# Attention and two MoE layers on one core: another order of the first loads, and the softmax sums' 1e-9 added by a tensor_reduce over pairs

## The chip, the cores and the metric

One core of a Trainium2 chip runs the whole program; nothing is shared with another core. The metric is the device time of one execution in microseconds. The kernel before takes 882.75 us, the median of three runs (882.33 to 882.92). The engines are named as in the profile: PE is TensorE (PEld its weight loads), DVE is VectorE, ACT is ScalarE, POOL is GpSimd, and SP is the queue from which all DMAs of this kernel are issued.

## The reference, cut to what matters

`q`, `k` and `v` are 4 x 8 x 576 x 64 (batch, heads, tokens, head width), in float32. For each batch and head two attentions are added: one over tokens averaged in fours, repeated back, and one local, in which a token sees the tokens less than 4 away. Both use the same softmax:

```python
s = s - np.max(s, axis=-1, keepdims=True)
a = np.exp(s)
a = a / (np.sum(a, axis=-1, keepdims=True) + 1e-09)
```

The sum, as 2304 rows of 512, goes through two layers; the weights come as 8-byte floats (512 x 2048 and 2048 x 512 for each layer):

```python
h = x @ w_in
g = h * (1.0 / (1.0 + np.exp(-h)))      # second layer: exp(-1.702 * h)
x = g @ w_out
```

## The kernel before

The work is cut into steps. Each step is a small function that issues a few instructions of one engine, with a name, an engine and what it reads and writes. The class `Plan` (from line 100) derives from that which steps must come before which. The order in which the steps are issued isn't worked out while building: it is the string `PLACES`, two characters a step, with the place of every step. `placed` (L135) refuses places that contradict the dependences and sorts the steps by them. So each engine's instruction order, and that of the SP queue, is the one written in `PLACES`; an engine runs its instructions in that order and waits where an operand isn't there. "Soft" edges (`plan.soft`) are no dependences: they are passed over in that test. A second table, `ON`, says for some steps on which engine they run.

**Attention.** The 2304 tokens are 8 blocks `m` of 288 (half a batch each). A unit `u` is one block and one pair of heads `hp`, so 32 units, four to a block. In order, a unit of the first blocks has these steps (from L1182; names as in the order, then the lines of the profile): `lk` and `lqqraw` load keys and queries (L1051, two DMAs each; in later batches L1048, four DMAs each), `vw` loads windows of the values (L1097) after POOL has zeroed the edge of the first one (`zvw0.0`), `KT` and `QT` form transposed and pooled keys and queries on TensorE with a helper tile `four` (L1131, L1195), ACT copies them (`KC` L1136 and L1138, `QC` L1199), `SC` makes the scores (L1219, L1226), `DM` and `LC` take maxima and cap the local scores (L1234, L1241, L1244), `LS` subtracts the maximum (L1250, on POOL or DVE), `DE` and `LE` take exponentials on ACT (L1256, L1260), `LU` sums the local ones (L1263), `RC` adds 1e-9 and takes reciprocals (L1267, L1268), `LN` and `DN` multiply by them (L1278 on POOL or DVE; L1275 on DVE or L1273 on ACT), `TP`, `TC` and `PT` transpose (L1285, L1289, L1293), `VP` and `VC` sum the values in fours (L1170, L1174), `AV` multiplies with the values (L1302, L1308), and `UC`, `XA`, `XM` copy, add and take the row's largest value (L1314 to L1326). In later batches DVE transposes keys and queries instead (`KX` L1141, `QX` L1204). The sums of one unit stand in a tile `smr` of 128 x 8: six columns from `LU`, two from the accumulators of `DE`.

**Weights of layer one** come in pairs of 1 MB (`ldst1in.c.j`, `ldst1out.c.j`, L524) into four staging tiles, 8 pairs in and 8 out. A pair is made into float32 by `ca` and `cz` on ACT (L326, L330), `cs` on DVE (a shift, L334), `sg` (the sign: on DVE a mask, L339, or on ACT a copy, L347) and two `cp` (the low words added, 512 columns each, on POOL or DVE, L351); `sps` and `spm` find its scale (L563, L578), and `hi` and `lo` split it into two float16 parts (L379, L383).

**Layers.** A block `m` is scaled and split (`rm`, `am`, `pw`, `xh`, `xl`; L769 to L784), then come eight pairs of h steps of 12 matmuls (L709), tanh and the rest on ACT and DVE (L721 to L734), and the output products (L842 in block 0, L814 after it). Layer two does the same for 9 blocks of 256 rows (L876 to L955); its sums `gs2` (L895 to L897) run on POOL or DVE as `ON` says. The weights of layer two are loaded and converted during layer one.

**Around the change.** The list `first` at the end (L1494) ties the first loads together with soft edges in the order that is written there. In `PLACES`, SP's order before is: weight pair in.0.0, queries 0, keys 0.0, queries 1, keys 0.1, value windows 0.0, pairs in.1.0 and in.0.2, queries 2, keys 0.2, windows 0.1, pair in.1.2, keys 0.3, pair in.2.0, and so on. TensorE begins with `QT0 KT0.0 QT1 SC0 KT0.1 VP0.0 SC1 TP0 AV0`. On POOL the initialisation (L997) sets constants to memory ahead of everything else.

## Time and profile before

| | |
|---|---|
| median of three runs | 882.75 us |
| the profiled execution | 885.88 us, its span 884.1 us |
| instructions | 23833 |
| PE busy | 859.8 us (97%) |
| DVE busy | 606.7 us (69%) |
| ACT busy | 465.4 us (53%) |
| POOL busy | 152.8 us (17%) |
| mean granted TensorE clock | 0.985 of full speed |

The profiled execution is one run by itself, timed with the profiler on. Its span goes from the first instruction to the last. Shares of busy time are averages over stages with different limits: PE is full from 132 us on and not before, so a stage must be read from its own stretch of the trace.

### The profile page before, as it was taken

Reading aid. Unit: us, or ns where it says so; the run is one execution under the profiler, and the core shown is the slowest. Engines: PE = TensorE matmul, PEld = TensorE weight load, DVE = VectorE, ACT = ScalarE, POOL = GpSimd, SP = SyncE. Lnnn points to the kernel's source line nnn. Section 1 sums busy time; section 2 is a strip of 40 time slices with the busy share of each in tenths; the row PEclk is TensorE's granted clock in tenths of the full one; section 3 lists DMA queues with packets and bytes.
Section 4 is the critical chain, followed back from the end, with each engine's and each line's share of the span. In section 5 each row is a group of like instructions: output and inputs, shape, how many; then the busy total and the mean of one; then the engine's idle time right before and its main releaser. Section 6 shows DMA issues by size and latency. Waiting matters only on the chain.

```text
span 884.1 us, 23833 instructions
## 1 busy us (share of the span) xinstructions
PE 859.8 (97%) x10212; PEld 718.1 (81%) x10212; DVE 606.7 (69%) x1342; ACT 465.4 (53%) x824; POOL 152.8 (17%) x184
## 2 busy tenths in 40 slices
...
GB/s 250 290 144 244 161 116 109 48 104 161 125 86 149 119 131 76 167 80 108 120 18 293 97 1 1 24 1 1 26 26 13 13 13 2 36 2 24 1 18 32
DMA packets 114990, 75.86 MB, mean 86 GB/s; under 512 B 94788, under 2 KB 100292, under 8 KB 113860
## 3 DMA queue, kind: packets, MB, share of 16 engines
...
## 4 chain that ended last, share of the span: by engine, by line
PE 84%; DVE 8%; ACT 4%; DMA 2%; SPq 1%; issue 1%; DVEq 0%; ACTq 0%
PE hps L876 20%; PE ops L814 19%; PE hps L709 19%; PE oy L955 10%; PE oz L955 5%; PE ox L955 2%; PE ul L1308 2%; PE sl L1226 1%; DMA kraw<-in_k_dram 1%; PE sl L1219 1%; PE ul L1302 1%; PE ops L842 1%; SPq L1051 1%; DVE wout L383 1%; DVE g L904 1%
## 5 line engine op out<-in xcount | busy, mean ns | idle before, releaser
L709 PE MATMUL hps<-xhl,win 128*128 128x288 f16 x1536 | 198.1, 287 | 0.9 <-DVE tg L724 0.9
L876 PE MATMUL hps<-xhl,win 128*128 128x256 f16 x1728 | 190.3, 273 | 0.0
L876 PEld LDWEIGHTS <-win 128*128 128x128 f16 x1728 | 169.1, 98 | 19.6
L709 PEld LDWEIGHTS <-win 128*128 128x128 f16 x1536 | 148.3, 98 | 38.3 <-issue 1.0
L814 PE MATMUL ops<-g,wout 128*128 128x288 f16 x1344 | 170.9, 286 | 0.0
L955 PEld LDWEIGHTS <-g 128*128 128x128 f16 x1512 | 147.7, 98 | 19.4 <-DVE g L904 1.3
L814 PEld LDWEIGHTS <-wout 128*128 128x128 f16 x1344 | 129.8, 98 | 32.7 <-issue 0.6
L888 ACT ACTIVATE tg<-hps,blk 128x512 f32<-128x512 f32 x72 | 49.5, 687 | 127.6 <-PE hps L876 116.3
L891 DVE SCALAR_TENSOR_TENSOR tg<-tg,hps 128x512 f32<-128x512 f32 x72 | 49.2, 683 | 59.9 <-ACT tg L888 59.9
L904 DVE SCALAR_TENSOR_TENSOR g<-tg,g 128x896 f16<-128x896 f32 x72 | 77.4, 1086 | 0.6 <-ACT g L901 0.3
L955 PE MATMUL oy<-wout,g 128*128 128x256 f16 x648 | 75.1, 272 | 0.0
L901 ACT ACTIVATE g<-tg 128x896 f16<-128x896 f32 x72 | 67.3, 944 | 14.5 <-DVE tg L897 10.4
L721 ACT ACTIVATE tg<-hps,blk 128x576 f32<-128x576 f32 x64 | 47.2, 737 | 42.3 <-PE hps L709 34.5
L351 POOL TENSOR_TENSOR cs<-cs,cz 128x512 int32<-128x512 int32 x32 | 41.9, 1316 | 154.9 <-DVE cs L334 54.8
L724 DVE SCALAR_TENSOR_TENSOR tg<-tg,hps 128x576 f32<-128x576 f32 x64 | 47.7, 747 | 27.3 <-ACT tg L721 27.2
L895 POOL TENSOR_TENSOR tg<-tg 128x128 f32<-128x128 f32 x14 | 9.7, 691 | 293.6 <-DVE tg L891 264.1
L933 ACT ACTIVATE o<-oy,blk 128x256 f32<-128x256 f32 x27 | 12.7, 472 | 73.6 <-PE oy L955 73.6
L734 DVE SCALAR_TENSOR_TENSOR g<-tg,gs,g 128x576 f16<-128x576 f32 x56 | 46.7, 839 | 6.1 <-ACT g L731 6.0
L326 ACT ACTIVATE st<-st 128x512 f32<-128x512 f32 (+1 forms) x48 | 39.6, 831 | 20.0 <-DMA st<-in_moe_w_out_dram 11.5
L731 ACT ACTIVATE g<-tg,gs 128x576 f16<-128x576 f32 x56 | 42.7, 769 | 13.1 <-DVE tg L724 12.5
L351 POOL TENSOR_TENSOR x<-x,z 128x512 int32<-128x512 int32 x26 | 37.4, 1453 | 49.3 <-DVE x L334 28.4
L939 DVE SCALAR_TENSOR_TENSOR o<-oy,blk,o 128x256 f32<-128x256 f32 x9 | 4.4, 484 | 59.0 <-PE oy L955 34.6
...
## 6 DMA issues: line engine op xcount, KB each, us to landing
...
```

The costliest lines, as they stand in the source:

```text
L351: eng.tensor_tensor(out=s, in0=s, in1=zget()[:, o], op=ALU.add)
L709: nc.tensor.matmul(o, T[w][:, kc, a, fc * P:(fc + 1) * P], T[xk][:, kc, b, :T_], start=(n == 0), stop=(n == 3 * KC - 1))
L721: ACT.activation(out=T[tg], in_=T[ps][:, :, :T_], func=AF.Tanh, scale=T["a" + bk][:, c:c + 1])
L724: DVE.scalar_tensor_tensor(out=T[tg], in0=T[tg], scalar=1.0, in1=T[ps][:, :, :T_], op0=ALU.add, op1=ALU.mult)
L734: DVE.scalar_tensor_tensor(out=T[g][:, 1], in0=T[tg], scalar=gs, in1=T[g][:, 0], op0=ALU.mult, op1=ALU.subtract)
L814: nc.tensor.matmul(o, w[:, j, a, dc * P:(dc + 1) * P], g[:, b, j % 2, :], start=(n == 0), stop=(n == 3 * NF - 1))
L876: nc.tensor.matmul(o, T[w][:, kc, a, fc * P:(fc + 1) * P], T[xk][:, kc, b, :], start=(n == 0), stop=(n == 3 * KC - 1))
L888: ACT.activation(out=four(), in_=T[ps][:, 0, :], func=AF.Tanh, scale=T["a" + bk][:, c:c + 1])
L891: DVE.scalar_tensor_tensor(out=four(), in0=four(), scalar=1.0, in1=T[ps][:, 0, :], op0=ALU.add, op1=ALU.mult)
L901: ACT.activation(out=T[g][:, 0], in_=T[tg], func=AF.Copy, scale=GS2)
L904: DVE.scalar_tensor_tensor(out=T[g][:, 1], in0=T[tg], scalar=GS2, in1=T[g][:, 0], op0=ALU.mult, op1=ALU.subtract)
L955: nc.tensor.matmul(T[bank[acc]], g[:, a, slot, :], w, start=first and p == p0 and i == 0, stop=prod in (2, 3, 4) and p == NF // 2 - 1 and ...
```

## The change

The change has three parts. `PLACES` is a new string, and the soft edges of the first loads are gone, so SP's order at the start is now: keys 0.0, queries 0, queries 1, keys 0.1, weight pairs in.0.2 and in.0.0, value windows 0.0, pair in.1.0, queries 2, keys 0.2, windows 0.1, queries 3, pairs in.1.2 and in.2.0, keys 0.3, and so on; the places of all 2670 steps are new with it. TensorE begins with `KT0.0 QT0 SC0 KT0.1 QT1 SC1 TP0 VP0.0 AV0`. The table `ON` is new: 88 steps change their engine, among them `sg`, `cp`, `LS`, `LN`, `DN` and `gs2` steps. And `RC` adds the 1e-9 otherwise: `smr` becomes 128 x 8 x 2 with 1e-9 in the second column of each pair, a tensor_reduce adds the pairs into a new tile `smi`, and the reciprocal is taken there. `LN` and `DN` read `smi`. Two more small memsets stand in the initialisation.

```diff
--- before.py
+++ after.py
@@ -23,17 +23,16 @@
 GS1, GS2 = 2.0 ** -15, 2.0 ** -19
 BAND = 4
 ON = {
-    "DVE": ("sg1.in.0.0 sg1.in.1.0 sg1.in.2.2 sg1.in.3.0 sg1.out.0.0 sg1.out.1.0 LS0 LN0 LN2 LS4 LN5 LN8 LS9 LS10 LN10 LS13 "
-             "LN13 LN14 LN16 LS17 LN17 LN18 LS19 LN19 LS20 LN20 LS21 LS22 LS23 LN23 LS24 LS27 LS28 LS29 LN29 LS31 gs2.0.1 "
-             "gs2.0.2 gs2.0.3 gs2.0.5 gs2.1.1 gs2.1.2 gs2.1.3 gs2.1.4 gs2.1.5 gs2.1.6 gs2.2.0 gs2.2.1 gs2.2.5 gs2.3.1 "
-             "gs2.3.2 gs2.3.3 gs2.3.4 gs2.3.5 gs2.3.6 gs2.4.1 gs2.4.2 gs2.4.3 gs2.4.4 gs2.4.5 gs2.4.6 gs2.5.0 gs2.5.1 "
-             "gs2.5.2 gs2.5.3 gs2.5.4 gs2.5.5 gs2.5.6 gs2.6.1 gs2.6.2 gs2.6.5 gs2.7.0 gs2.7.1 gs2.7.2 gs2.7.3 gs2.7.4 "
-             "gs2.7.5 gs2.7.6 gs2.8.0 gs2.8.1 gs2.8.2 gs2.8.3 gs2.8.4 gs2.8.5 gs2.8.6"),
-    "POOL": ("cp1.in.0.0a cp1.in.0.2b cp1.in.1.0a cp1.in.1.0b cp1.in.1.2b cp1.in.2.0a cp1.in.2.2a cp1.in.2.2b cp1.in.3.0a "
-             "cp1.in.3.0b cp1.in.3.2a cp1.in.3.2b cp1.out.0.0a cp1.out.0.0b cp1.out.0.2a cp1.out.1.0a cp1.out.1.0b "
-             "cp1.out.1.2a cp1.out.1.2b cp1.out.2.0a cp1.out.2.2a cp1.out.2.2b cp1.out.3.0a cp1.out.3.0b cp1.out.3.2a "
-             "cp1.out.3.2b"),
-    "ACT": ("DN2 DN4 DN5 DN6 DN7 DN8 DN11 DN12 DN13 DN15 DN17 DN20 DN21 DN22 DN30 DN31"),
+    "DVE": ("sg1.in.0.0 sg1.in.0.2 sg1.in.1.0 sg1.in.1.2 sg1.in.2.0 sg1.in.2.2 sg1.in.3.2 sg1.out.0.2 sg1.out.2.0 LS0 LN0 "
+             "LS2 LN2 LS3 LN3 LS4 LN4 LS8 LS9 LN9 LN10 LS11 LS12 LN13 LS14 LS15 LS17 LS19 LN19 LN22 LN23 LN24 LN27 LS28 LS29 "
+             "LS30 LN30 LN31 gs2.0.0 gs2.0.2 gs2.0.3 gs2.0.5 gs2.1.1 gs2.1.2 gs2.1.3 gs2.1.4 gs2.1.5 gs2.1.6 gs2.2.0 gs2.2.1 "
+             "gs2.2.2 gs2.2.3 gs2.2.4 gs2.2.5 gs2.2.6 gs2.3.1 gs2.3.2 gs2.3.3 gs2.3.4 gs2.3.5 gs2.3.6 gs2.4.1 gs2.4.5 "
+             "gs2.5.1 gs2.5.2 gs2.5.3 gs2.5.4 gs2.5.5 gs2.5.6 gs2.6.1 gs2.6.2 gs2.6.3 gs2.6.4 gs2.6.5 gs2.6.6 gs2.7.1 "
+             "gs2.7.5 gs2.8.1 gs2.8.2 gs2.8.3 gs2.8.4 gs2.8.5 gs2.8.6"),
+    "POOL": ("cp1.in.0.2a cp1.in.1.0b cp1.in.1.2b cp1.in.2.0b cp1.in.2.2a cp1.in.2.2b cp1.in.3.0b cp1.out.0.0b cp1.out.0.2a "
+             "cp1.out.0.2b cp1.out.1.0a cp1.out.1.0b cp1.out.1.2a cp1.out.1.2b cp1.out.2.0a cp1.out.2.0b cp1.out.2.2a "
+             "cp1.out.3.0a cp1.out.3.0b cp1.out.3.2a cp1.out.3.2b"),
+    "ACT": ("DN3 DN4 DN5 DN6 DN7 DN8 DN9 DN10 DN11 DN12 DN13 DN14 DN15 DN16 DN22 DN24 DN25"),
 }
 
 
@@ -46,46 +45,46 @@
 PLACES = (
-    "0206040307050k0h0L0V00090n111u010a080J0q0U0Y180f0H0S0N0W0X1o1s0e0w0B0F0Q101C1I0K1r1v1y1z1B1R1V0T1Z1L262g2i2r2x1q2d2n2h2G2o2L2R1S2N2Z2Q"
...
+    "0006010204030t0f160S05090y1d1w080z0w0I0H0U111b070N0Y0T18101h1v0b0R1c1e1f1g1l1p0X1t1K1x231C272b121N1R1T1Y2c2j2q1k2f292m2A2o2E2P2a2Q2U2V"
...
 )
@@ -1011,9 +1010,11 @@
         T["qTs"] = [ac.tile([P, HALF + PD], F32, name=f"qT{i}") for i in range(2)]
         for t in T["qTs"]:
             POOL.memset(t[:, HALF:], 0.0)
-        T["smr"] = [ac.tile([P, 8], F32, name=f"smr{i}") for i in range(2)]
+        T["smr"] = [ac.tile([P, 8, 2], F32, name=f"smr{i}") for i in range(2)]
+        T["smi"] = [ac.tile([P, 8], F32, name=f"smi{i}") for i in range(2)]
         for t in T["smr"]:
-            POOL.memset(t, 1.0)
+            POOL.memset(t[:, :, 0], 1.0)
+            POOL.memset(t[:, :, 1], 1e-9)
         T["vsum"] = ac.tile([P, 3, PD], F32, name="vsum")
         POOL.memset(T["vsum"], 0.0)
         T["four"] = ac.tile([P, TT + 2 * QB], F32, name="four")
@@ -1254,28 +1255,28 @@
             T[sr] = T["smr"][u % 2]
             for hh in range(2):
                 ACT.activation(out=T[pd][:, hh, :], in_=sd()[:, hh, :], func=AF.Exp, bias=T[nmx][:, hh:hh + 1],
-                               scale=SCD if blocked(m) else 1.0, accum_out=T[sr][:PD, 6 + hh:7 + hh])
+                               scale=SCD if blocked(m) else 1.0, accum_out=T[sr][:PD, 6 + hh, 0:1])
 
         def lexp():
             ACT.activation(out=scu(), in_=scu(), func=AF.Exp, scale=0.125)
 
         def lsum():
-            DVE.tensor_reduce(out=T["smr"][u % 2][:, 0:6], in_=scu(), axis=AX.X, op=ALU.add)
+            DVE.tensor_reduce(out=T["smr"][u % 2][:, 0:6, 0], in_=scu(), axis=AX.X, op=ALU.add)
 
         def rec():
 
-            DVE.tensor_scalar(out=T["smr"][u % 2], in0=T["smr"][u % 2], scalar1=1e-9, scalar2=None, op0=ALU.add)
-            DVE.reciprocal(out=T["smr"][u % 2], in_=T["smr"][u % 2])
+            DVE.tensor_reduce(out=T["smi"][u % 2], in_=T["smr"][u % 2], axis=AX.X, op=ALU.add)
+            DVE.reciprocal(out=T["smi"][u % 2], in_=T["smi"][u % 2])
 
         def dnorm():
             if on(f"DN{u}", "DVE") == "ACT":
                 for hh in range(2):
-                    ACT.activation(out=T[pd][:, hh, :], in_=T[pd][:, hh, :], func=AF.Copy, scale=T[sr][:PD, 6 + hh:7 + hh])
+                    ACT.activation(out=T[pd][:, hh, :], in_=T[pd][:, hh, :], func=AF.Copy, scale=T["smi"][u % 2][:PD, 6 + hh:7 + hh])
                 return
-            DVE.tensor_tensor(out=T[pd], in0=T[pd], in1=T[sr][:PD, 6:8].unsqueeze(2).to_broadcast([PD, 2, 2 * PD]), op=ALU.mult)
+            DVE.tensor_tensor(out=T[pd], in0=T[pd], in1=T["smi"][u % 2][:PD, 6:8].unsqueeze(2).to_broadcast([PD, 2, 2 * PD]), op=ALU.mult)
 
         def lnorm():
-            (POOL if on(f"LN{u}", "POOL") == "POOL" else DVE).tensor_tensor(out=scu(), in0=scu(), in1=T["smr"][u % 2][:, 0:6].unsqueeze(2).to_broadcast([P, 6, 32]), op=ALU.mult)
+            (POOL if on(f"LN{u}", "POOL") == "POOL" else DVE).tensor_tensor(out=scu(), in0=scu(), in1=T["smi"][u % 2][:, 0:6].unsqueeze(2).to_broadcast([P, 6, 32]), op=ALU.mult)
 
         def dtr():
             T[tps] = bank1("tps")
@@ -1339,7 +1340,7 @@
         add(f"LS{u}", on(f"LS{u}", "POOL"), 0.58 if on(f"LS{u}", "POOL") == "POOL" else dve(192) + 0.02, lsub, lock=on(f"LS{u}", "POOL") == "DVE", r=[], w=[sc])
         add(f"LE{u}", "ACT", act(192), lexp, w=[sc])
         add(f"LU{u}", "DVE", dve(192), lsum, r=[sc, (sr, "d")], w=[sr])
-        add(f"RC{u}", "DVE", 0.34, rec, r=[(sr, "d")], w=[sr])
+        add(f"RC{u}", "DVE", 0.35, rec, r=[(sr, "d")], w=[sr])
         add(f"LN{u}", on(f"LN{u}", "POOL"), 0.55 if on(f"LN{u}", "POOL") == "POOL" else dve(192) + 0.02, lnorm, lock=on(f"LN{u}", "POOL") == "DVE", r=[sr], w=[sc])
         nby = on(f"DN{u}", "DVE")
         add(f"DN{u}", nby, dve(4 * PD) if nby == "DVE" else 2 * act(2 * PD, 1), dnorm, r=[sr], w=[pd], lock=nby == "DVE")
@@ -1490,15 +1491,6 @@
             s.deps.setdefault(s3, False)
 
 
-    by = {s.name: s for s in plan.steps}
-    first = []
-    for hp, p in zip(range(NHP), ("0.0", "0.2", "1.0", "1.2")):
-        first += [f"lk0.{hp}", f"lqqraw{hp}", f"vw0.{hp}", "ldst1in." + p]
-    first += ["ldst1in." + p for p in ("2.0", "2.2", "3.0", "3.2")]
-    for c in range(NC):
-        first += [f"ldst1out.{c}.0", f"lqqraw{NHP + c}", f"ldst1out.{c}.2"]
-    for a, b in zip(first, first[1:]):
-        plan.soft.append((by[a], by[b]))
     order = plan.placed(PLACES)
     es0 = ExitStack()
     with es0, es1, es2:
```

## Rows read from the trace of the kernel before

**Rows 1.** Busy time by stretches (start:end, length, engines' us and instructions, granted clock, DMA).

```profile
0.00:21.95 21.95, 14.18 (x156) 12.54 (x157) 6.64 (x25) 10.55 (x19) 2.55 (x25) 1.00 1.06 250
21.95:36.00 14.05, 12.98 (x222) 11.68 (x223) 9.97 (x26) 9.30 (x17) 4.30 (x5) 0.64 1.09 297
36.00:61.40 25.40, 20.09 (x320) 18.02 (x319) 22.29 (x59) 25.40 (x43) 10.72 (x9) 0.74 0.59 188
61.40:132.00 70.60, 64.90 (x1053) 50.43 (x1047) 68.12 (x160) 61.70 (x105) 33.05 (x28) 0.97 0.73 173
132.00:868.00 736.00, 734.86 (x8357) 614.38 (x8355) 498.36 (x1073) 356.70 (x638) 102.20 (x119) 1.00 0.24 66
48.00:55.10 7.10, 3.46 (x79) 2.81 (x77) 5.96 (x18) 7.10 (x15) 4.48 (x5) 0.98 0.72 206
55.10:65.60 10.50, 10.47 (x146) 8.09 (x145) 8.89 (x27) 10.16 (x18) 4.23 (x4) 0.53 0.62 150
```

**Rows 2.** The timeline from 0 to 24 us (start, length, engine, line, instruction).

```profile
0.74 0.44 SPq L524 DMA_DIRECT2D st<-in_moe_w_in_dram  x1
1.24 0.96 SPq L1051 DMA_DIRECT2D qraw<-in_q_dram  x2
...
4.21 0.18 DVE L1029 TENSOR_SCALAR four<-four 128x24 f32<-128x24 f32 x1
...
6.88 1.61 PE L1195 MATMUL qps<-four,qraw 96*128 96x120 f32 x6 [6.88 <-DMA qraw<-in_q_dram]
...
21.95 0.48 PE L1302 MATMUL ul<-pdT,vd 72*64 72x72 f32 x8 [0.89 <-ACT vd L1174]
```

**Rows 3.** DMA issues of the keys (count, size, us from issue to landing).

```profile
kraw<-in_k_dram SPq DMA_DIRECT2D x48, 72.0 KB, 4.3
```

**Rows 4.** Groups by line (shapes, count, busy us, mean ns, idle before).

```profile
L1275 DVE TENSOR_TENSOR pd<-pd,smr 72x288 f32<-72x288 f32 x16 | 9.1, 569 | 0.3
...
L347 ACT ACTIVATE z<-st 128x1024 f16<-128x1024 f32 x10 | 13.7, 1369 | 0.1
...
L339 DVE TENSOR_SCALAR z<-st 128x1024 uint16<-128x1024 uint16 x6 | 4.5, 747 | 0.0
...
L351 DVE CUSTOM_DVE_ANT_0 x<-x,z 128x1024 uint16<-128x1024 uint16 x6 | 4.6, 761 | 0.0
...
L1250 DVE TENSOR_TENSOR sc<-sc,mx 128x192 f32<-128x192 f32 x16 | 5.9, 367 | 0.3
...
L1234 DVE TENSOR_REDUCE nm<-sl 72x2 f32<-72x288 f32 x32 | 14.2, 443 | 15.0 <-PE sl L1226 15.0
...
L1241 DVE TENSOR_TENSOR sc<-sl,cap 128x192 f32<-128x192 f32 x32 | 11.0, 344 | 14.4 <-PE sl L1226 13.5 <-ACT pd L1256 0.8
...
L334 DVE TENSOR_SCALAR x<-st 128x1024 int32<-128x1024 int32 x16 | 12.5, 788 | 0.6 <-ACT st L326 0.6
```

**Rows 5.** Single lines of DVE (durations in ns: least/median/longest, first and last start).

```profile
L1263 DVE TENSOR_REDUCE smr<-sc x32: 308/344/354, 15.8 to 422.4; 128x6 f32<-128x192 f32 x32
L773 DVE TENSOR_REDUCE blk<-rm x17: 110/154/163, 57.5 to 788.9; 128x1 f32<-128x4 f32 x17
L1267 DVE TENSOR_SCALAR smr<-smr x32: 152/172/1250, 18.3 to 423.4; 128x8 f32<-128x8 f32 x32
L1278 DVE TENSOR_TENSOR sc<-sc,smr x14: 345/356/2100, 19.1 to 402.5; 128x192 f32<-128x192 f32 x14
```

**Rows 6.** The timelines of DVE and of POOL around 107 us.

```profile
107.12 1.25 DVE L1267 TENSOR_SCALAR smr<-smr 128x8 f32<-128x8 f32 x1
...
104.98 3.35 POOL L351 TENSOR_TENSOR x<-x,z 128x512 int32<-128x512 int32 x2 [3.86 <-ACT z L347]
```

**Rows 7.** Busy time of L1267 alone (DVE busy, count).

```profile
61.40:132.00 70.60, 2.54 (x6) 0.97 0.73 173
```

**Rows 8.** The timeline of PE, two h steps of twelve matmuls.

```profile
61.41 3.06 PE L709 MATMUL hps<-xhl,win 128*128 128x288 f16 x12
...
71.93 1.64 PE L709 MATMUL hps<-xhl,win 128*128 128x288 f16 x12
```

More of the change, by code (lines that the diff above doesn't have):

```diff
@@ new lines @@
+    "3130383d282J2B332N3b3u3y15171o1B1E1L1J1P1U212t2L2x2z2M2W373R3h3j3v454y502i3r3U3B473J3P4d4i353F3z403N4o4v4s4A39424g4a5g5l5t5r5z3A4O5R4T"
+    "5Z5T5W696f4j4Z53585b6m6A6w6N4n596b5m6K6s6y6S6Y5p6l6Z6D726H6P7d7v65787G7l7K7q7x7Q7V5h5U6g6r6x6G62646O776U706X797e7n7w7F7E7M7T7Z80878Q0a"
+    "0d0C0L0c0e0g0i0j0l0k0m0p0q0r0s0A0D0v0O0W0Z140h0o1q1y0n0u0x0E0B0G0F0J0K0M0Q0P1j1n0V1A1D1F1G191i1W24131a1m1r1s1z1u1I1O1Q1S1X22261V2h2p2s"
+    "2G1M202v2H1H1Z252e2g2k2n2r2u2w2C2y2D2I2F2K2O2R2S2X32363e3n3l3W4c3Q636o7j8s2d2l2Z3m2T2Y343c3f3i3k3p3t3x3C3D3H3L3K3T41444x3g3o3q3G3E3O3I"
@@ new lines @@
+    "3S3V3Z434e4l4r4w4F4N4P6d464b4f4p4B4u4E4K4X5a5f5d5j5o5u5D5M5P5S4R52565q5e5x5k5v5E5I5O5N5V5X5Y61686c6h6k6p747C7J8hcz543a6j493s5Q7B4W6a8M"
+    "847p6B99905G5A674I4G4J6e6n6v6q6C6E6V737u7b7h7m7y7H7R7U9i4k4C8k5C5H6J7f6T7o898c8d8g8w8i8n8q8x8F8J8L9Q7c7z8Y7P7Y828p8b8t8e8r8y8z8G8K8S8V"
+    "949c9l9p9s8m8H9r8C8D8O8T958X9a9b9d9e9g9n9v9x9t9C9G9I9Ja1a8adanawatak888E8R9O8P929K9V9Sa09U9Wa4a6abaaaeazaiaDaHaKaM9k9ma7agauaxaCaOaTaY"
+    "bib1b6babjbobubxbCa9alaSb9b5bhbbbfbnbpc2bwbHbKc5c6cccecwarbEbGbNbIbRbMbObVbXc0cdchcncacpcucvcycOcScUcZdmd0hP7g9Xbdc19Zc9cWb3bvdAcsclaX"
```

70 lines of the change are left out of this document (31 added, 39 removed).

## The prediction

> **What bounds the kernel now.** I read the busy time by stretches first [rows 1], then the first microseconds in order of time [rows 2, 3], then the groups by line [rows 4], and last the spread of the instructions that the new sums touch [rows 5 to 7]. From 132 to 868 us TensorE is busy for 734.86 of 736.00 us [rows 1]. The changed lanes of units 12 to 31 and of layer two lie in that stretch; TensorE's own work hides them, and the most they could uncover is the 1.1 us that it still waits. So the change is decided before 132 us.
>
> There are three stretches. Up to 21.95 us, where the first attention-times-value matmul starts, the DMA engines are full (share 1.06) and DVE works 6.64 us; TensorE starts only at 6.88 us, when the first query tile has landed behind a weight pair of 1 MB issued ahead of it [rows 1, 2]. From 36 to 61.4 us, where the first h matmul starts, ACT is busy for 25.40 of 25.40 us, DVE for 22.29 and TensorE for 20.09 [rows 1]. From 61.4 to 132 us DVE is busy for 68.12 of 70.60 us, and TensorE waits 5.7 us in all [rows 1]. Thus the early bound is loads, then ACT, then DVE, and TensorE after that.
>
> **The loads.** The first eleven loads are the same set in both orders: three query tiles, three key tiles, two value windows and three weight pairs. Only their order inside the first 22 us differs, and with the DMA engines full to 36 us [rows 1] the set lands no sooner. What changes is that the keys and queries of two units, eight DMAs on SP, go ahead of the first 1 MB pair. TensorE then begins with the key product. It can start when its helper tile "four" is written, on which the last small instruction ends at 4.39 us [rows 2], or when the keys land: the second key DMA would be issued where the second issue of the queue now stands, at 1.24 us [rows 2], and a key DMA takes 4.3 us to landing [rows 3], which gives 5.5 us. That median is one among other traffic, and here nothing is ahead in the queue, so I take 5.0 us, 1.9 us sooner; the bounds are 4.4 (2.5 us sooner) and 6.88 (nothing).
>
> Most of that is given back. Before, the copies of the first two query products lie beside key matmuls. After, the order on TensorE is keys, query, scores for unit 0, and for unit 1 the query comes last again, so each scores step waits for the copy of a product that TensorE has just made. The one such wait that the trace shows cost 0.89 us [rows 2]; at 0.75 us each, two cost 1.5 us. The TensorE steps up to 21.95 us are otherwise the same nine. Stretch one: -1.9 + 1.5 = **-0.4 us**, between -1.6 and +1.0.
>
> The weight conversions that used to run from about 6 us wait for pairs issued some 4 us later. ACT, which does the first of them, is busy for 10.55 of the first 21.95 us [rows 1] and covers that; without the cover one pair's two passes would come late. Further on SP issues the third output-weight pair ahead of two key tiles (eight DMAs) and one value tile. The keys of the second batch are first turned by DVE much later in the new order too, so I cost this at nothing; if it showed, it would be as a DVE turn waiting for a key tile. The zeroing of one value window moves behind the POOL initialisation, and two small memsets are added there: nothing, as SP reaches that window's load later.
>
> **The lanes up to 61.4 us.** ACT loses four sign copies (L347, 1369 ns) and gains one: -4.1 us [rows 4]. That is off the engine that bounds the stretch. But DVE gains them as sign masks (L339, 747 ns): four more, +3.0 us. It takes over five halves of the low-word add from POOL and gives back two (L351, 761 ns): +2.3 us. Two subtractions (L1250, 367 ns) and one local normalisation (0.36 us at its median [rows 5]) come from POOL: +1.1 us. One direct normalisation goes each way. Last, unit 4's maximum, cap, cap maximum and subtraction now stand ahead of the split of the first x tile, and one shift of an output weight behind it: 0.44 + 0.34 + 0.34 + 0.37 - 0.79 = +0.7 us [rows 4, 5] (the cap maximum by the reduce of the same width). DVE has 7.1 us more to do by 61.4 us. Its idle time from 21.95 to 61.4 us is 4.1 + 3.1 = 7.2 us [rows 1], beside what unit 0 frees earlier. So ACT stops being the bound and DVE becomes it, with next to no slack. I take **0 us** for this stretch: the 4.1 us off ACT can be cashed only as far as DVE comes early. Bounds: -4.1 (all of ACT's relief) and +4.4 (under rival one).
>
> **The lanes from 61.4 to 132 us.** DVE, the bound here, has one sign mask less (-0.75), two halves of the add more (+1.5), two local normalisations out and one in (-0.36), one subtraction in (+0.37), one direct normalisation out to ACT (L1275, -0.57), and the 0.7 us that moved ahead: **-0.5 us** [rows 4, 5].
>
> **The sums.** L1267 adds 1e-9 with a tensor_scalar; its replacement is a tensor_reduce that reads 16 numbers a partition and writes 8. The nearest rows are the reduce of 4 numbers (median 154 ns) and the reduce of 192 (344 ns) [rows 5]; 1 ns a number puts it at 0.17 us. L1267 has a median of 172 ns too, so the arithmetic costs the same. But it has stretched to 1250 ns, where L1263 has never exceeded 354 [rows 5]: at 107.12 us it lasted 1.25 us and ended with a POOL add that had run since before [rows 6]. From 61.4 to 132 us the six of them take 2.54 us [rows 7]; six at 0.17 are 1.02. So up to 1.5 us leave DVE. The wait needn't vanish, though: a DVE multiply with two inputs has stretched as well (L1278, median 356, longest 2100 ns [rows 5]), and if the POOL add is still running, the next such instruction waits instead. Between the two stands at least the reciprocal, and the POOL add runs down meanwhile; I take 1.2 of the 1.5 us, nearer to the row of the reduces that never stretched: **-1.2 us**, bounds 0 and -1.5.
>
> The Trainium skill, SBUF — State Buffer, section Who interferes with whom, has a rule for this that cuts both ways: on this chip a tensor_reduce never contends with GpSimd, while a DVE instruction with two SBUF inputs waits for a GpSimd instruction that reads SBUF. The trace agrees with both halves: 354 against 2100 ns at the longest. By the second half the wait is only handed on, and the gain in the sums would be near 0 in place of 1.2 us.
>
> **Sum.** -0.4 + 0 - 0.5 - 1.2 = -2.1 us. The profiled execution took 885.88 us around a span of 884.1; it stands 3.1 us above the median of 882.75. Taken from that median: 880.65, so **880.6 us**. About 0.2%, 1.8 us, is what a measurement of this kernel can tell from no change.
>
> **Rival one: DVE takes over before the first h matmul (slower).** Place: from the shift of weight pair 1.2 to the split of the first x tile. Of the added steps these stand behind that point: three masks, one half of the add net, one subtraction, one normalisation and the 0.7 us of unit 4, in all 2.24 + 0.76 + 0.37 + 0.36 + 0.7 = 4.4 us [rows 4, 5]; DVE's idle time from 36 us on is 3.1 us [rows 1]. For: those idle pieces are waits for ACT and TensorE and can't all be filled. Against: unit 0 comes earlier and POOL's slow adds no longer stand ahead of the conversions. Price: with none of that idle time of use, the first h matmul comes 4.4 us later, less the 1.7 us of the last stretch and the 0.4 of the first: +2.3, 885.0 us. It decides once that matmul is more than 3.9 us late (2.1 + 1.8).
>
> **Rival two: nothing to measure.** The first eleven loads are one set, TensorE's early start is eaten by the copies, and the wait of the sums is handed to the next two-input instruction. Then -0.4 - 0.5 = -0.9 at best and some lateness on DVE against it: 882.4 us. That is also the case in which the new sums change nothing.
>
> **Rival three: the clock.** From 55.1 to 65.6 us the granted clock is 0.53, close to the lower level of 1.2 GHz; before that, from 48 to 55.1 us, it was 0.98 (2.4 GHz) and TensorE was busy for 3.46 of 7.10 us only [rows 1]. With ACT relieved, those pauses may shrink and the clock hold. The twelve matmuls of an h step took 3.06 us there and 1.64 later [rows 8]; the stretch holds 10.47 us of TensorE work, and all of it at that ratio would give back 4.9 us. I take 3 for the part that the clock limits; with the forecast's sum that makes 877.6 us. Against: more DVE work means waits of TensorE elsewhere.
>
> **How the numbers follow.** Forecast 0.32 and clock 0.12: faster 0.44. Nothing: 0.31. DVE takes over: 0.25. The range is 876.5 to 885.5: it takes in the clock case below and the DVE case above, and leaves out the ends of several bounds at once. As cases of both signs hold the chance, the forecast's own range is 878.8 to 881.0.
>
> **What would show it.** Right: TensorE's first matmul near 5 us, with two new waits of 0.7 to 0.8 us ahead of scores; the first attention-times-value matmul within 1 us of 21.95; the first h matmul within 1.5 us of 61.4; ACT with pauses from 36 to 61.4 us and DVE with less idle; the sums' instruction at 0.17 us in every one of 32 cases; TensorE's waits from there to 132 us down from 5.7 to about 4. Wrong: a first h matmul over 3 us away from 61.4 either way (then DVE or the clock decided), a reduce over 0.4 us, or new waits of TensorE after 132 us.

## The result, and the profile after

The changed kernel takes 887.73 us, the median of seven runs (885.39 to 890.61), beside 882.92 us for seven runs of the kernel before on the same chip (882.33 to 885.68): a ratio of 1.0055, 95% interval 1.0040 to 1.0069. It is 4.8 us slower, where 2.1 us less was forecast; it lies beyond the upper end of the range (885.5) and on the side of rival one.

The profiled execution took 887.04 us around a span of 885.2. That of before stood 3 us above its median, so a second profile of it (run a1: 883.34 us median, profiled span 882.2) is used beside the first from here on.

The busy time by stretches, changed kernel (columns as in [rows 1]):

```profile
0.00:21.95 21.95, 15.80 (x220) 13.74 (x221) 9.51 (x32) 10.66 (x23) 5.28 (x29) 1.00 0.96 238
21.95:36.00 14.05, 10.48 (x177) 9.12 (x177) 12.31 (x29) 9.35 (x19) 3.36 (x2) 0.88 1.10 270
36.00:61.40 25.40, 17.77 (x312) 15.26 (x312) 24.68 (x59) 22.46 (x39) 8.11 (x5) 0.70 0.79 224
61.40:132.00 70.60, 66.44 (x1042) 51.80 (x1041) 67.84 (x161) 59.20 (x99) 25.81 (x25) 0.94 0.70 166
132.00:868.00 736.00, 733.60 (x8348) 613.94 (x8347) 491.08 (x1056) 358.56 (x643) 114.22 (x134) 1.00 0.24 66
```

Against [rows 1], ACT from 36 to 61.4 us went from 25.40 to 22.46 us and DVE from 22.29 to 24.68: the full engine changed, as the lanes say. TensorE lost 2.3 us of work in that stretch. And behind 132 us it now waits 2.40 us in place of 1.14.

The timeline of TensorE in the changed kernel, its start and four marks:

```profile
4.29 2.89 PE L1132 MATMUL kps<-four,kraw 96*128 96x120 f32 x12 [4.29 <-DVE four L1029]
...
9.06 0.76 PE L1220 MATMUL sl<-kd,qT 64*72 64x144 f32 x4 [0.61 <-ACT qT L1200]
...
15.27 0.76 PE L1220 MATMUL sl<-kd,qT 64*72 64x144 f32 x4 [0.64 <-ACT qT L1200]
...
20.16 0.48 PE L1303 MATMUL ul<-pdT,vd 72*64 72x72 f32 x8 [0.51 <-ACT vd L1175]
...
62.06 3.06 PE L708 MATMUL hps<-xhl,win 128*128 128x288 f16 x12
...
133.92 3.10 PE L841 MATMUL ops<-g,wout 128*128 128x288 f16 x24 [0.72 <-DVE x L855]
...
136.86 1.63 PE L708 MATMUL hps<-xhl,win 128*128 128x288 f16 x12
...
156.36 0.47 PE L1220 MATMUL sl<-kd,qd 64*72 64x144 f32 x4 [0.86 <-DVE xf L1324]
```

The start answers to [rows 2] (4.29 against 6.88 us), the matmul with the values too (20.16 against 21.95), the first h step to [rows 8] (62.06 against 61.41).

Four times divide the span: the first matmul with the values (AV), the first h matmul, the second block's first h matmul, the end. All are read from the timelines; stretches are their differences.

| kernel | AV | AV to first h | first h to second block | second block to end | span |
|---|---|---|---|---|---|
| before, first profile | 21.95 | 39.46 | 75.63 | 747.06 | 884.10 |
| before, second profile (a1) | 22.42 | 37.18 | 75.60 | 746.98 | 882.18 |
| changed | 20.16 | 41.90 | 74.80 | 748.37 | 885.23 |
| changed, old sums (a3) | 21.37 | 42.85 | 74.79 | 749.51 | 888.52 |

Against the second profile of before the changed kernel gains 2.3 us up to AV, loses 4.7 from there to the first h matmul, gains 0.8, and loses 1.4 at the end: +3.1 us in the spans.

The last three differences aren't loss and gain alone, since two of the marks have other work on either side in the two orders. The new order does the scores of unit 5 ahead of the first h matmul, the old one behind it; the new order does one unit's value products behind the second block's first h matmul, the old one ahead of it. TensorE in the changed kernel, and below it in a1:

```profile
60.68 0.76 PE L1220 MATMUL sl<-kd,qT 64*72 64x144 f32 x4 [0.78 <-ACT qT L1200]
...
138.42 0.48 PE L1303 MATMUL ul<-pdT,vd 72*64 72x72 f32 x8
138.83 0.71 PE L1309 MATMUL ul<-PT,vw 32*64 32x24 f32 x48
...
62.02 0.47 PE L1219 MATMUL sl<-kd,qT 64*72 64x144 f32 x4
62.42 0.62 PE L1226 MATMUL sl<-kT,qT 64*32 64x32 f32 x48
...
134.15 0.48 PE L1302 MATMUL ul<-pdT,vd 72*64 72x72 f32 x8
```

In a1 these scores take 62.97 - 62.02 = 0.95 us and the value products 135.20 - 134.15 = 1.05 us. So 0.95 of the 4.7 us is work that only stands earlier, the gain of 0.8 stands against 2.0 us less work and is a loss of 1.2, and 1.05 of the last 1.4 us is work that only stands later. What TensorE waits in a stretch says the same without this shift (stretches as above, changed kernel and a1; TensorE's busy time is the first figure behind the length):

```profile
20.16:62.06 41.90, 30.59 (x595) 26.43 (x595) 39.26 (x91) 34.26 (x58) 12.25 (x8) 0.77 0.91 239
62.06:136.86 74.80, 69.91 (x1031) 54.46 (x1027) 71.87 (x170) 61.26 (x107) 27.66 (x26) 0.95 0.67 155
...
22.42:59.60 37.18, 30.67 (x543) 27.43 (x543) 32.15 (x83) 34.77 (x59) 14.84 (x13) 0.75 0.84 244
59.60:135.20 75.60, 70.68 (x1139) 54.68 (x1135) 72.94 (x174) 62.53 (x110) 34.20 (x30) 0.97 0.69 165
```

From AV to the first h matmul TensorE waits 11.3 us in place of 6.5, from there to the second block 4.9 in both (there the granted clock is 0.95 in place of 0.97), and behind it 5.0 in place of 4.4. So most of the loss is in the stretch for which I had put 0 us. What is late there is DVE. Its groups by line from 20 to 62 us, the changed kernel (count, busy us, mean ns, idle before):

```profile
L333 DVE TENSOR_SCALAR x<-st 128x1024 int32<-128x1024 int32 x7 | 7.2, 1027 | 0.0
L382 DVE SCALAR_TENSOR_TENSOR win<-x,bin,win 128x1024 f16<-128x1024 f32 x5 | 6.7, 1346 | 0.0
L350 DVE CUSTOM_DVE_ANT_0 x<-x,z 128x1024 uint16<-128x1024 uint16 x7 | 5.8, 833 | 0.2
L338 DVE TENSOR_SCALAR z<-st 128x1024 uint16<-128x1024 uint16 x6 | 5.4, 899 | 0.1
```

and the same groups in the second profile of before:

```profile
L383 DVE SCALAR_TENSOR_TENSOR win<-x,bin,win 128x1024 f16<-128x1024 f32 x5 | 7.0, 1421 | 0.6 <-ACT win L379 0.6
L334 DVE TENSOR_SCALAR x<-st 128x1024 int32<-128x1024 int32 x9 | 6.4, 725 | 0.6 <-ACT st L326 0.6
L351 DVE CUSTOM_DVE_ANT_0 x<-x,z 128x1024 uint16<-128x1024 uint16 x4 | 3.2, 805 | 0.0
L339 DVE TENSOR_SCALAR z<-st 128x1024 uint16<-128x1024 uint16 x3 | 2.3, 751 | 0.0
```

The counts are about those of the prediction: three masks and three additions more by 62 us (and two shifts fewer). But a shift takes 1027 ns on the mean, where it took 725, and a mask 899 for 751. The timelines show why; DVE and, below it, POOL in the changed kernel:

```profile
25.38 0.68 DVE L350 CUSTOM_DVE_ANT_0 x<-x,z 128x1024 uint16<-128x1024 uint16 x1
25.98 1.75 DVE L333 TENSOR_SCALAR x<-st 128x1024 int32<-128x1024 int32 x1
...
44.39 1.75 DVE L333 TENSOR_SCALAR x<-st 128x1024 int32<-128x1024 int32 x1
...
25.63 1.55 POOL L350 TENSOR_TENSOR x<-x,z 128x512 int32<-128x512 int32 x1 [4.03 <-DVE z L338]
...
42.21 3.37 POOL L350 TENSOR_TENSOR x<-x,z 128x512 int32<-128x512 int32 x2 [11.86 <-DVE z L338]
```

POOL's addition ends at 25.63 + 1.55 = 27.18 us, the shift at 27.73; at 42.21 + 3.37 = 45.58, the shift at 46.14. Both shifts end 0.55 us behind the addition, about as if they had begun with its end. For both, TensorE's order puts the next `sps` product behind the shift, and with it what follows: scores after the first, sums of the values after the second. TensorE's waits up to 70 us, changed kernel (total us, times, longest):

```profile
PE sps L562 <- DVE x L333: 5.5, 3, 2.7
PE kps L1132 <- DVE four L1029: 4.3, 1, 4.3
```

In the second profile of before the first of these is 1.7 us, and the second is a wait for queries of 7.4 us.

For all DVE instructions that start from 20 to 62 us I took what each lasts beyond the lower quartile of its form (the quartile over both first profiles). The sum, called the excess below, is 5.1 us in the changed kernel and 2.2 and 2.5 in the two profiles of before.

The new sums' instruction (ns: least/median/longest, first and last start), which answers to L1267 in [rows 5]:

```profile
L1268 DVE TENSOR_REDUCE smi<-smr x32: 127/170/171, 13.0 to 419.4; 128x8 f32<-128x16 f32 x32
```

### The profile page after: what moved, and what is told of

It is laid out like the page before. It is cut to its first block, busy times and chain, and to the rows that moved or that the text cites. A ratio compares the mean times of both kernels' runs of the same rounds, so it can differ in the third digit from the quotient of the medians.

```text
span 885.2 us, 23848 instructions
## 1 busy us (share of the span) xinstructions
PE 858.0 (97%) x10212; PEld 716.0 (81%) x10212; DVE 607.4 (69%) x1336; ACT 462.0 (52%) x823; POOL 156.8 (18%) x194
## 4 chain that ended last, share of the span: by engine, by line
PE 84%; DVE 13%; ACT 2%; issue 1%; POOL 0%; DVEq 0%; POOLq 0%; ACTq 0%
PE hps L875 19%; PE ops L813 19%; PE hps L708 18%; PE oy L954 11%; PE oz L954 5%; PE ox L954 3%; PE sl L1227 2%; PE ul L1309 2%; DVE wout L382 1%; PE sl L1220 1%; PE ul L1303 1%; DVE g L733 1%; DVE g L903 1%; DVE x L333 1%; PE tps L1286 1%
## 5 line engine op out<-in xcount | busy, mean ns | idle before, releaser
L708 PE MATMUL hps<-xhl,win 128*128 128x288 f16 x1536 | 200.2, 289 | 0.3 <-DVE tg L723 0.2
L954 PE MATMUL oy<-wout,g 128*128 128x256 f16 x648 | 75.1, 273 | 0.0
L894 POOL TENSOR_TENSOR tg<-tg 128x128 f32<-128x128 f32 x18 | 11.5, 638 | 347.3 <-DVE tg L890 347.3
L350 POOL TENSOR_TENSOR cs<-cs,cz 128x512 int32<-128x512 int32 x32 | 41.9, 1313 | 125.6 <-DVE cz L338 49.3
L350 POOL TENSOR_TENSOR x<-x,z 128x512 int32<-128x512 int32 x21 | 30.3, 1457 | 49.7 <-ACT z L346 24.7
L1257 ACT ACTIVATE pd<-sl,nm 72x144 f32<-72x144 f32 x64 | 23.4, 370 | 18.4 <-DVE nm L1237 13.7
```

Of the source, the lines that this page charges most:

```text
L350: eng.tensor_tensor(out=s, in0=s, in1=zget()[:, o], op=ALU.add)
L708: nc.tensor.matmul(o, T[w][:, kc, a, fc * P:(fc + 1) * P], T[xk][:, kc, b, :T_], start=(n == 0), stop=(n == 3 * KC - 1))
L954: nc.tensor.matmul(T[bank[acc]], g[:, a, slot, :], w, start=first and p == p0 and i == 0, stop=prod in (2, 3, 4) and p == NF // 2 - 1 and ...
```

## The experiments

The changes of order in these runs are moves in `PLACES`; they are shown as lists of steps.

### The parts alone (a1 to a4)

Run a1 is the kernel before, unchanged.

> The kernel before, unchanged, for a second profile of it. Its profiled execution above took 885.88 us where its seven runs have a median of 882.92, so 3 us of an unlucky stretch may be in that one trace. All theories: a ratio of 1.000 within 0.002, and a profiled run near 882.9 us. What it is to show is where the first profile had lost its 3 us, and so which stretch of the changed kernel is really longer.

Measured: 883.34 us, ratio 0.9998 (0.9985 to 1.0011), span 882.2. Its first h matmul is at 59.60 us, 1.8 us ahead of that of the first profile, which had 27 us at the lower clock level against 24; behind that matmul the two run alike. So 62.06 us in the changed kernel is 2.5 us late, not 0.65, with unit 5's scores ahead of it.

Run a2 is the kernel before with the sums of the change:

```diff
-            DVE.tensor_scalar(out=T["smr"][u % 2], in0=T["smr"][u % 2], scalar1=1e-9, scalar2=None, op0=ALU.add)
+            DVE.tensor_reduce(out=T["smi"][u % 2], in_=T["smr"][u % 2], axis=AX.X, op=ALU.add)
```

> The kernel before with the pairs and the tensor_reduce alone; order and lanes as before. My prediction: 1.2 us less (0 to 1.5), so 881.7 us, ratio 0.9986. Theory 'the sums hand the wait on' (LN on POOL or DVE starts earlier and meets more of POOL's work): 0 to +2 us, up to 885. Theory 'the loss is in the order and the lanes': 881 to 883 us here.

Measured: 883.19 us, ratio 0.9988 (0.9976 to 1.0000). Run again as d4, it gave no gain (below).

Run a3 is the opposite part: order, loads and lanes of the change with the line that a2 removes.

> The changed kernel's order, first loads and lanes, with the old tensor_scalar for the 1e-9. If order and lanes carry the loss: 887.7 + 0 to 1.2 = 887.7 to 889 us, ratio 1.0055 to 1.007. If the new sums carry it: 882 to 884 us.

Measured: 887.73 us, ratio 1.0045 (1.0029 to 1.0060). Order and lanes carry the loss; the sums carry no part that shows, and save nothing that shows in the new order.

Run a4 takes order and lanes from the change up to the second block's first h step and from before behind it. It has the old sums, and so have b1 to b4.

> The new order and the new lanes for every step that the changed kernel places ahead of the second block's first h step (about the first 137 us: attention of the first blocks, the loads and most of the layer one weights); from there the old order and lanes; the sums are the old ones. Theory 'startup' (rival one: DVE becomes the bound before the first h matmul, 61 us): all of the loss is here, 886 to 888 us. Theory 'later' (waits behind 132 us that the new order makes): 882 to 883.5 us, and the loss shows when the other half is run.

Measured: 885.90 us, ratio 1.0019 (1.0007 to 1.0031). AV is at 20.08, the first h matmul at 61.56 us, as in the changed kernel; the second block to the end takes 746.6 us, as before. Something is lost in the head, less than half of the whole.

### Cuts at other places (b1 to b4)

Each joins the new order up to one step with the old one behind it (b3 the other way round):

```
 b1: new up to AV                              | old behind
 b2: new up to the first h matmul              | old behind
 b3: old up to the second block's first h step | new behind
 b4: new up to block 4's first h step          | old behind
```

> The changed kernel's order only for the steps ahead of its first matmul with the values (the first 50 places: first loads, the keys and queries of two units); the rest, and all lanes of later steps, as before; old sums. The profile of the changed kernel has that matmul at 20.16 us where the kernel before has it at 21.95 and 22.42. If the earlier start were kept: 1.8 us less, 882.1 us against 883.9, ratio 0.998. My prediction gave the start 0.4 us, so 883.5 us. Theory 'the start is lost again, because the weights come later and the shifts for sps are what TensorE waits for next': 883.9 us or up to 1 us more.

> The new order and lanes up to the first h matmul (about 62 us), old from there; old sums. With the head up to 137 us the loss was 1.7 us (885.9 against 883.9). Theory 'DVE's two late shifts' (TensorE waits 5.3 us in sps for cs instead of 1.7 to 2.1, and the first h matmul is 2 us later than in the second profile of before): the whole 1.7 us, 885.5 to 886 us. Rival 'the loss is between 62 and 137 us' (transposes and second low-clock stretch at 112 us): 883.5 to 884.3 us.

> The other half of the head kernel: old order and lanes up to the second block's first h step, the new ones from there; old sums. From that matmul to the end the two profiles of before take 747.0 us, the changed kernel 748.4, and with the old sums 749.5. So 883.9 + 1.4 to 2.5 = 885.3 to 886.4 us, ratio 1.0016 to 1.0028. Rival 'the head's 1.7 us pushes the rest into new waits' (the two don't add): 883.5 to 884.5 us here.

> New order and lanes up to the first h step of block 4 (near 300 us), old from there; old sums. If the rest's loss is the waits at 134 and 156 us (0.7 ops for the evacuation x, 0.9 scores for xf) and those up to 300 us: nearly all of the loss, 887 to 887.7 us. If it lies in the second layer's lanes (gs2 on DVE or POOL): 886 us.

Measured: b1 887.11 us, ratio 1.0043 (1.0029 to 1.0057); b2 889.33, 1.0071 (1.0048 to 1.0094); b3 884.15, 1.0003 (0.9991 to 1.0015); b4 894.26, 1.0127 (1.0107 to 1.0146). Three of the four lie outside what either theory expected, and a4, with a cut between those of b2 and b4, is better than both. A joint has a price of its own: one order leaves late what the other needs early. In b4, for one, the stretch from 200 to 300 us holds 4.8 us of TensorE waits, where no whole order has more than 1. So cuts can't divide this loss; of the four only b3 is clean in its trace: head as before (first h matmul at 59.93 us), second block to the end 748.2 us, 1.2 us longer than in a1 with the same work behind the mark.

From b1 I drew a theory all the same. In it the old lanes follow the new first loads, and it is as slow as the whole, with 41.5 us from AV to the first h matmul; so the first weight pair, issued at 5.4 us in place of 0.7, might be the cause.

### The first weight pair back in front, and the old lanes (c1 to c4)

```diff
 SP, c1 and c2 against the change:
-lk0.0 lqqraw0 lqqraw1 lk0.1 ldst1in.0.2 ldst1in.0.0 vw0.0
+ldst1in.0.0 lk0.0 lqqraw0 lqqraw1 lk0.1 ldst1in.0.2 vw0.0
 ACT, c2 alone:
-KC0.0 QC0 DE0 LE0 KC0.1 QC1 cz1.in.0.0 ca1.in.0.0
+cz1.in.0.0 ca1.in.0.0 KC0.0 QC0 DE0 LE0 KC0.1 QC1
```

> The changed kernel with one load moved: weight pair in.0.0 is issued ahead of keys 0.0 (at 0.7 us, as before) instead of sixth (5.4 us). Nothing else moves. Theory 'late weights' (the DMA engines are full from 4 us to 61 us and carry 0.4 to 0.7 MB less by 8 to 36 us when only small loads stand at the head; at some 300 GB/s that is 1.5 to 2.5 us by which each later pair comes late): 887.7 - 2 = 885.5 to 886.2 us, although TensorE starts some 2.5 us later. Rival 'DVE is the bound from 20 us on, by lanes and order': 887.5 to 889 us.

> As the run above, and the first conversions cz and ca of that pair are ACT's first steps, as before (there at 6.7 us, in the changed kernel at 15.3 us, though ACT idles 7.4 of its first 10 us in it). Theory 'late weights': 2 to 4 us less than the changed kernel, 884 to 885.7 us. If only the load's place matters it equals the run above; if neither matters, 887.5 us or more.

Measured: c1 890.56 us, ratio 1.0079 (1.0062 to 1.0097); c2 892.18 us, 1.0101 (1.0081 to 1.0121). Both are slower than the changed kernel, so the theory of the late weights falls. In c1 TensorE waits for the first keys (its waits up to 70 us, columns as above):

```profile
PE kps L1131 <- DMA kraw<-in_k_dram: 7.8, 1, 7.8
```

AV comes at 23.91, the first h matmul at 65.39 us: 3.75 and 3.3 us later than in the changed kernel. In the new order a late start is passed on whole; the early start is real there, and the 41.5 us between the two marks stay.

Run c3 gives `sg` and `cp` of layer one the engines that they had before, in the new order.

> The changed kernel with the sign and low-word steps of layer one's weights (sg, cp) on the engines that they had before: more sg on ACT, more cp on POOL. Order, loads and sums as changed. Theory 'lanes' (DVE idles 0.5 us of 45 to 61 us and TensorE waits 5.3 us for its shifts): 1 to 3 us less, 885 to 886.7 us. Theory 'late weights': no gain from it, 887 us or more, since the order was chosen for the new lanes.

Measured: 888.47 us, ratio 1.0052 (1.0037 to 1.0067). No gain. With more additions on POOL again, DVE's excess is 3.7 us, and AV to first h is 41.2 us; these two are from a profiled execution of 884.43 us, 4 us below the run's median.

Run c4 joins the new head (cut of a4), the new sums and the move of c2.

> A candidate: new order and lanes up to 137 us (885.9 alone), old behind it, the new sums (-1.1 alone), and the first pair with its conversions first. If the three add: 885.9 - 1.1 - 2 to 4 = 881 to 883 us, below before (883.5). If the early start and the early weights exclude each other: 884 to 885 us.

Measured: 891.31 us, ratio 1.0092 (1.0073 to 1.0111): some 6 us above what was expected and 5 above a4, as c2 was 4 above the changed kernel.

### POOL's additions taken away (d1, d2)

Run d1 leaves out the additions that POOL does ahead of the first h matmul: seven half pairs of the weights go without their low words, and DVE's steps stay as they are. Run d2 does the same in the kernel before, with its eight.

```diff
-    lambda by=by, o=o: cp(POOL if by == "POOL" else DVE, o)
+    (lambda: None) if "cp" + nm + x in OFF else (lambda by=by, o=o: cp(POOL if by == "POOL" else DVE, o))
```

> The changed kernel without the seven low-word additions (cp) that POOL does ahead of the first h matmul; those half pairs go without their low words. DVE's own work stays the same. In the changed kernel's profile DVE's instructions from 20 to 62 us are 5.1 us longer than the same forms elsewhere, nearly all of it beside these additions (a shift of 0.68 us takes 1.75 us and ends 0.55 us after POOL's addition ends); in the kernel before it is 2.2 to 2.5 us. Theory 'DVE held by POOL': the excess falls to under 2 us, the first h matmul comes 2.5 to 4 us earlier, 884 to 885.5 us against 887.9. Rival 'the weights come late' (loads) or 'there is simply more work left': within 1 us of the changed kernel.

> The control: the kernel before without the eight low-word additions that POOL does there ahead of the first h matmul; those half pairs go without their low words. Here ACT is the full engine from 36 to 61 us and DVE's excess is 2.2 to 2.5 us. Theory 'DVE held by POOL': 0 to 1.5 us less, 882 to 883.5 us, less than half of what the changed kernel gains.

Measured: d1 883.86 us, ratio 0.9998 (0.9985 to 1.0012); d2 883.83 us, ratio 1.0000 (0.9992 to 1.0008). The same removal gives the changed kernel some 4 us, all that it had lost, and it gives the kernel before nothing. In d1 the first h matmul is at 59.50 us and the excess 0.5 us (in d2 1.1). It isn't the lateness of POOL's results that the removal takes away: in the changed kernel's waits from 20 to 62 us none of another engine ends with POOL. The shift that lasted 1.75 us, in DVE's timeline of d1:

```profile
26.11 0.69 DVE L334 TENSOR_SCALAR x<-st 128x1024 int32<-128x1024 int32 x1
...
44.52 0.69 DVE L334 TENSOR_SCALAR x<-st 128x1024 int32<-128x1024 int32 x1
```

and DVE's groups from 20 to 62 us:

```profile
L383 DVE SCALAR_TENSOR_TENSOR win<-x,bin,win 128x1024 f16<-128x1024 f32 x5 | 6.4, 1274 | 0.0
L351 DVE CUSTOM_DVE_ANT_0 x<-x,z 128x1024 uint16<-128x1024 uint16 x9 | 6.1, 680 | 0.2
L334 DVE TENSOR_SCALAR x<-st 128x1024 int32<-128x1024 int32 x8 | 5.6, 699 | 0.1
L339 DVE TENSOR_SCALAR z<-st 128x1024 uint16<-128x1024 uint16 x6 | 4.5, 746 | 0.0
```

Every mean is back at its form's plain value. Not all of the 4 us is DVE's: the mean granted clock of d1's runs is 0.991, that of the changed kernel's and of before's 0.987. That is 7.4 us less at the lower level (15.6 against 23.0, from (1 - clock) x 2 x span); over the 35 runs of before beside d1, a microsecond less at that level went with 0.2 us less time, so some 1.5 us may be the clock's. In the two profiles d1 gains 2.7 us from AV to the first h matmul (39.20 us in place of 41.90) and 2.5 us from there to the second block (72.31 in place of 74.80), where TensorE waits more (5.7 us in place of 4.9) but the granted clock is 1.00 in place of 0.95; behind that it loses 1.0. The clock's share came with the same removal, but not from DVE's time alone.

### Two candidates (d3, d4)

Run d3 is the kernel before with the new sums and an earlier start.

```diff
 SP:
-ldst1in.0.0 lqqraw0 lk0.0 lqqraw1 lk0.1
+lqqraw0 lk0.0 ldst1in.0.0 lqqraw1 lk0.1
 ACT:
-cz1.in.0.0 ca1.in.0.0 QC0 KC0.0
+QC0 KC0.0 cz1.in.0.0 ca1.in.0.0
```

> A candidate: the kernel before with the new sums, queries 0 and keys 0.0 issued ahead of the first weight pair, and that pair's two ACT conversions behind the first copies of queries and keys. Everything else as before. It has the early start of the changed kernel without its later order. Theory 'the early start itself is worth its time where the rest is as before': first matmul near 5 us, 1 to 2 us less than the kernel with the sums alone (883.1), 881 to 882 us. Rival 'the start is swallowed by the full ACT or by weights that come a microsecond later': 883 to 884 us.

> The new sums alone once more, beside the candidate on the same chip, since the first answer (ratio 0.9988, 0.9976 to 1.0000) reaches to no change. Forecast: 0.9986, 0.6 to 1.5 us less.

Measured: d3 884.10 us, ratio 1.0003 (0.9992 to 1.0013); d4 883.77 us, ratio 1.0003 (0.9994 to 1.0013). In d3 TensorE waits 4.5 us for `four` at the start but then 2.7 us for the second queries and 3.2 us for `vd`, and AV is at 22.80 us: the start is swallowed. A part of that is ACT's own: in before its ACT_TABLE_LOAD of 1.28 us ran at 0.73 us, in d3 at 6.24 us, between the first query product and its copy. For the sums, a2 and d4 together leave between nothing and 1 us. Their traces agree with a small gain: first h to second block takes 74.9 and 75.1 us in them, 75.6 in both profiles of before.

### The later part, and the additions on DVE (e1, e2)

Run e1 is d1 up to the second block's first h step, with the old order and lanes behind.

> The changed kernel without POOL's seven low-word additions (those half pairs go without their low words, as in the run before), and with the old order and lanes from the second block's first h step on. From that step to the end the changed order took 748.2 to 749.5 us in five profiles, the old one 746.6 to 747.5. Theory 'the later part costs its own 1.2 to 2.4 us': 883.6 - 1.2 to 2.4 = 881.2 to 882.4 us, below the kernel before. Rival 'those waits only follow from a late head': 883.6 us, no gain.

Measured: 882.68 us, ratio 0.9989 (0.9976 to 1.0001), 1.2 us below d1. From the second block on it takes 747.3 us, d1 749.4, of which 1.05 us are the value products that only d1 has behind the mark. So the later part costs about a microsecond, though the intervals of the two runs touch.

Run e2 computes all that the changed kernel does. The seven additions run on DVE:

```diff
-    "POOL": ("cp1.in.0.2a cp1.in.1.0b cp1.in.1.2b cp1.in.2.0b cp1.in.2.2a cp1.in.2.2b cp1.in.3.0b cp1.out.0.0b cp1.out.0.2a "
+    "POOL": ("cp1.out.0.0b cp1.out.0.2a "
...
```

> The whole changed kernel, but the same seven additions run on DVE, where one takes 0.68 us. That adds 4.8 us to DVE between 20 and 62 us and takes away the stretching beside POOL (5.1 us there, about 0.5 left without the additions). Theory 'DVE held by POOL': the two cancel, first h matmul within 1.5 us of the changed kernel's 62 us, 886.5 to 889 us: what POOL takes over there it charges to DVE again. Rival 'DVE's own work is what counts': 4 to 5 us more, 891 to 893 us.

Measured: 885.22 us, ratio 1.0016 (1.0003 to 1.0030): better than both theories, and 2.5 us below the changed kernel. The first h matmul is at 60.33 us. DVE's groups from 20 to 62 us:

```profile
L348 DVE CUSTOM_DVE_ANT_0 x<-x,z 128x1024 uint16<-128x1024 uint16 x15 | 10.0, 688 | 0.0
L380 DVE SCALAR_TENSOR_TENSOR win<-x,bin,win 128x1024 f16<-128x1024 f32 x5 | 6.4, 1276 | 0.0
L331 DVE TENSOR_SCALAR x<-st 128x1024 int32<-128x1024 int32 x7 | 4.8, 687 | 0.7 <-ACT st L323 0.7
L336 DVE TENSOR_SCALAR z<-st 128x1024 uint16<-128x1024 uint16 x6 | 4.5, 746 | 0.0
```

The four groups hold 33 instructions in 25.7 us; in the changed kernel, 25 in 25.1 us. Eight more additions cost DVE 0.6 us net. TensorE waits 3.0 us for shifts, not 5.5.

No kernel that computes everything came out measurably below the kernel before.

## Why the prediction was wrong, point by point

- **The loads: the right sign, undersized.** TensorE started at 4.29 us (5.0 forecast, 4.4 the bound, which was set by the last instruction on `four` and was 0.1 us too late). The two new waits ahead of the scores came, at 0.61 and 0.64 us (0.75 forecast). AV came 1.8 to 2.3 us earlier, where I had put 0.4 with an end at 1.6. That this set of loads can come in either order at no other cost is not settled: c1 and c2 show only that the pair in front costs the start.
- **The lanes up to 61.4 us: the step that failed.** I put 0 us. The mechanism up to the engine was right: ACT got pauses and DVE became the bound. But I counted DVE's added steps by their mean durations [rows 4], and the slack by idle time. The runs show that durations don't stay: with POOL's additions beside them, the shift, the mask and DVE's own additions last up to 1.07 us longer. The excess rose from 2.2 to 2.5 us to 5.1, which is over half of the 4.7 us between AV and the first h matmul. d1 against d2 shows it as the cause, and e2 shows it from the other side: without POOL's additions that stretch is 39.2 us in both, where the changed kernel has 41.9. That fewer additions stayed on POOL (seven for ten by 62 us) had looked like relief; what counts is which DVE instruction stands beside them. Of the rest, some 2 us, 0.95 is unit 5's scores, which I hadn't counted as TensorE's work ahead of that matmul; what is left may be the steps moved to DVE, as counted, but no run took these alone. b1 is late there for another reason, which stays open: its excess is 2.0 us, and ACT is full again (25.37 of 25.40 us from 36 to 61.4 us).
- **Rival one** named the engine, the place and the sign, and its 885.0 us is nearest to what came. Its price was made from counts alone (4.4 us for moved steps), so it reached the size by another way; and I held against it that "POOL's slow adds no longer stand ahead of the conversions".
- **The rule beside the sums.** The row was there: a one-input DVE instruction stretched to 1.25 us beside a POOL addition [rows 6]. The Trainium skill, SBUF — State Buffer, section Who interferes with whom, says that a tensor_scalar from SBUF in its two-port forms also takes the port pair that DVE shares with GpSimd, that the pair is locked for a whole instruction, and that the one that issues later waits. I applied the rule to the sums only, and not to the masks and shifts that the new lanes put beside the additions. Here the trace agrees with it: the shift of 0.68 us took 1.75 us and ended 0.55 us behind the addition.
- **The sums: mis-sized.** Each reduce lasts 0.17 us as forecast (127 to 171 ns). The term was 1.2 us; the runs leave 0 to 1 us in the old order and nothing that shows in the new one. The traces show that half of the wait is handed on. From 61.4 to 132 us the six instructions take 0.98 us in a2 where they took 2.27 in a1, but the two multiplications of DVE behind them (L1278 in a1) take 2.24 us in place of 1.61, in a2 as in d4: 0.66 of 1.29 us stays. One such place, a1 and below it a2:

```profile
105.27 1.26 DVE L1267 TENSOR_SCALAR smr<-smr 128x8 f32<-128x8 f32 x1
...
106.80 0.36 DVE L1278 TENSOR_TENSOR sc<-sc,smr 128x192 f32<-128x192 f32 x1
...
104.24 0.17 DVE L1269 TENSOR_REDUCE smi<-smr 128x8 f32<-128x16 f32 x1
...
104.69 0.99 DVE L1280 TENSOR_TENSOR sc<-sc,smi 128x192 f32<-128x192 f32 x1
```

- **Lanes from 61.4 to 132 us and TensorE's waits there:** the number came, the gain didn't. TensorE waits 70.60 - 66.44 = 4.2 us (about 4 forecast), but from the first h matmul to the second block the time is 0.8 us less with 2.0 us less work, where the two terms forecast 1.7 us less for the same work; the granted clock there is 0.95, in a1 0.97. DVE's excess there didn't fall (6.1 us from 61.4 to 132 us, in a1 5.5).
- **After 132 us: the second step that failed.** I had said that the changed lanes uncover 1.1 us at the most, and put nothing for what they add. The two new waits in the timeline above (0.72 and 0.86 us, both for DVE) are of that size. Eight profiles with the new later order take 748.2 to 749.5 us from the second block on, eleven with the old 746.4 to 747.9, but seven of the eight have 1.05 us more work there. TensorE's waits behind the mark are 5.0 to 6.0 us in the eight and 4.1 to 5.2 in the eleven. In time, e1 below d1 puts it at about 1 us and b3 alone at 0.3 us, with an interval from -0.8 to +1.3.
- **The clock:** no part in the change that the means show, 0.987 for both kernels' runs; by stretches it differs, as the item on 61.4 to 132 us says. Rival three needed ACT's relief to keep TensorE from pausing; TensorE paused more.

What stays open: with the old sums the head alone cost 1.7 us and the later part alone 0.3, the whole 4.0. The two don't add, and the seven runs of the changed kernel spread over 5.2 us; one profile of each can't show which waits come and go.
